# First batch's inverse transform: channel pairs (c, c+128) and whole 128-column weights in its last stage

## The chip, the cores and the metric

The kernel runs on one core of one Trainium2 chip. Inside a core, TensorE (PE) multiplies matrices and writes its results to PSUM; VectorE (DVE) and ScalarE (ACT) work element by element and carry PSUM results to SBUF; GpSimd (POOL) does side work; SyncE (SP) and POOL issue most of the DMAs. The metric is device microseconds of one execution. Before the change three executions took 790.2, 790.48 and 791.0 us, median 790.48 us.

A PE weight load (LDWEIGHTS, shown as its own engine PEld) puts the *stationary* operand into the array; the matmul that follows streams the *moving* operand through it. Both are read from SBUF, each partition along its own row, with a stride that the program chooses.

## The reference, cut to what matters

```
X = np.fft.rfft(x, axis=1)                 # x: 8 batches x 3008 positions x 256 channels
Y = X * (filt_r + 1j * filt_i)
y = np.fft.irfft(Y, n=3008, axis=1)        # per channel: a filter along the positions
h = y.reshape(24064, 256) @ w_in           # 256 -> 2048
s = np.sin(alpha * h)
out = (h + s * s / alpha) @ w_out          # 2048 -> 256
```

## The kernel before, in words

Positions are split as 3008 = 94 x 32, 94 rows (two interleaved sets of 47) by 32 columns that the code calls `n`. The forward transform of a batch is two matrix stages with a turn between them, then comes the product with the filter, then two inverse stages with a turn back between them. The result `y` is held in fp16 as two blocks of 128 channels (`cb` = 0, 1) by positions, and the second half of the kernel consumes it in chunks of 512 positions: `hidden(k, jb)` (L500) does two matmuls (one for each `cb`) with `w1`, ACT takes a sine (L510), DVE makes the snake activation (L511); `project(k, u)` (L515) multiplies by `w2` and stores. 48 such chunks, 12 for every two batches, carry most of the time.

Batches 1 to 7 are spread in small pieces between those matmuls by a list of due times (`put`, L557, and `slot`, L597); their turns go through DRAM by DMA. Batch 0 has to be there before the first chunk, so it is done on the chip by itself, in a written order (L361 to L492). This is the part that the change touches:

- First stage (L368 to L378): 16 matmuls; DVE and ACT in turn copy each result from PSUM into `t1_0`. The copy regroups the 256 channels as 128 pairs, because the turn moves 32-bit words, two fp16 channels at a time. Before the change a pair is (2c, 2c+1).
- Turn (`turn`, L383): four DVE transposes of 32x32 blocks of 32-bit words, into two halves `t2_0[0]` and `t2_0[1]` (`hc` = 0, 1), each with 64 pairs. `t2_0[0]` is the memory `t4_h[0]`. The memory `t4_h[1]` meanwhile holds `e1_0`, the second table of the inverse. In a turned tile the two members of a pair are neighbours, and the next pair of the same `n` or frequency lies 64 elements (128 bytes) further on.
- Second stage (`forward_0`, L399), 12 calls of four matmuls, K=128, 128x128 weights `d_t`, moving operand 128 columns read straight from the turned tile: 64 pairs of neighbours, 128 bytes apart. ACT copies the result to `xf0`.
- Product (`product_0`, L409), one DVE instruction per call on 128 neighbouring channels of the filter, for both filter parts.
- Third stage (`inverse_0`, L416), eight matmuls per call, contiguous moving operands, PSUM pool `fps` with two buffers; ACT copies the result into `g_0` with `(k c) -> c k`, so that here columns c and c+64 of the half become a pair.
- Turn back (`turn_back`, L388), two DVE transposes, of half 0 and then of half 1, into `t4_0[0]` and `t4_0[1]`. As pairs are (c, c+64) inside one half of 128 channels, `t4_0[cb]` has exactly the 128 channels of the block `cb`.
- Last stage (`last(u)`, L246): 16 calls `u`, each for four values of `n` and one `cb`. For batch 0 each `n` takes two matmuls, k = 0 and 1, with 64 weight columns each (stride 128 bytes in SBUF), whose outputs go to PSUM partitions 0 to 63 and 64 to 127. PSUM comes from `fps` again, so two calls can be open. ACT or DVE copies the result (128x376) into `y`.

The order around it, L474 to L492: `reciprocal(rec)` is issued on DVE right behind the two transposes; PE does the two last alpha broadcasts (`spread_alpha`, L295), `warm_pe(2)` (matmuls on zeros that keep the array busy), `last(0)` and `last(2)` (both of `cb` = 0, which need only the first transpose), `warm_pe(3)`, then `last(1)` and `last(3)` (`cb` = 1, which need the second transpose). Then `hidden(0,0)`, `hidden(0,1)` and the transpose of `rec` on PE (L611), whose copy `rec_t` (L612) scales `w2`. Calls 4 to 15 of `last` come in pairs (`last_two`, L262) at the due times 1, 3, 4.5, 6, 14 and 16, between the hidden matmuls of the first three chunks (L571). No DMA is touched by the change.

Of the kernel before, what the change touches and what calls it, by code (L numbers as in the profile page):

```python
# [9 lines left out]
FP16 = mybir.dt.float16  # L10
# [4 lines left out]
ALU = mybir.AluOpType  # L15
# [3 lines left out]
B, S, C = 8, 3008, 256  # L19
# [43 lines left out]
def kernel(  # L63
# [10 lines left out]
    nc = tc.nc  # L74
# [21 lines left out]
    cpool = pool("consts", 1)  # L96
# [12 lines left out]

    wf_t = cpool.tile([NR, NK], FP16)  # L110
    t1_h = [cpool.tile([128, 16, C], FP16, name=f"t1_h{i}") for i in range(2)]
    t4_h = [cpool.tile([128, 16, C], FP16, name=f"t4_h{i}") for i in range(2)]

    def by_half(t):

# [8 lines left out]
    for h in range(2):  # L124
        nc.sync.dma_start(out=x32[:, 4 * C * h:4 * C * h + 4 * C],
                          in_=bass.AP(tensor=x.tensor, offset=x.offset + 4 * h * C, ap=[[32 * C, 96], [1, 4 * C]]))
# [4 lines left out]
    wi0_t = cpool.tile([128, NR], FP16)  # L131
    filt_t = cpool.tile([128, 2, NS, C], FP16)
# [23 lines left out]
    def evac(dst, src, on_act=None):  # L156
        flip[0] = (flip[0] + 1) % 3
        if flip[0] if on_act is None else on_act:
            marks["act"] = nc.scalar.copy(out=dst, in_=src)  # L159
        else:  # L160
            marks["dve"] = nc.vector.tensor_copy(out=dst, in_=src)  # L161

    class Spectral:
# [82 lines left out]
        def last(self, u, on_act=None):  # L246
            ch, rest = divmod(u, 4)
            half, cb = divmod(rest, 2)
            n0 = 8 * ch + 4 * half
            ps = fps.tile([128, 4, 128], FP32, name=f"pd_{self.b}_{u}", tag="f")  # L250
            psv = ps.rearrange("p a b -> p (a b)")[:, 0:4 * NR].rearrange("p (a r) -> p a r", r=NR)
            for i in range(4):
                if self.b == 0:
                    for k in range(2):
                        nc.tensor.matmul(out=psv[64 * k:64 * k + 64, i, :], lhsT=t4_0[cb][:, n0 + i, :, k],  # L255
                                         rhs=wi0_t, start=True, stop=True)
                else:
                    nc.tensor.matmul(out=psv[:, i, :], rhs=wi_t, start=True, stop=True,  # L258
                                     lhsT=t4_h[ch // 2][0:NK, n0 % 16 + i, cb * 128:cb * 128 + 128])
            evac(y[:, cb, self.b % 2, n0:n0 + 4, :], psv, on_act)  # L260
# [9 lines left out]
    al = cpool.tile([16, 128], FP32)  # L270
# [33 lines left out]
    for g in range(2):  # L304
        gs = slice(12 * g, 12 * g + 12)
        for k, filt in enumerate((filt_r, filt_i)):
            for q in range(2):
                if (g, k, q) == (0, 1, 1):
# [3 lines left out]
                    out=f_t[k][64 * k + 32 * q:64 * k + 32 * q + 32, gs, :],  # L312
# [8 lines left out]
    def pairs(t):  # L321

        return t.rearrange("p a (b s k) -> p s (a b) k", s=32, k=2)

    t1_0 = vpool.tile([128, 32, C], FP16, name="t1_0", tag="v")
    t2_0 = [t4_h[0], vpool.tile([128, 16, C], FP16, name="t2_0", tag="v")]
    for hc in range(2):
        nc.vector.memset(pairs(t1_h[hc])[:, NS:32], 0.0)
    t1_0, t2_0, g_0, t4_0 = pairs(t1_0), [pairs(t) for t in t2_0], [pairs(t) for t in t1_h], [pairs(t) for t in t4_h]
    rec = cpool.tile([16, 128], FP32)  # L330
    rec_t = cpool.tile([128, 16], FP32)
# [17 lines left out]
    def warm_pe(n):  # L349

        warmed.append(n)
        ps = hps.tile([128, 512], FP32, name=f"warm_{len(warmed)}", tag="h")
        for i in range(n):
            nc.tensor.matmul(out=ps, lhsT=idle[:, 0:128], rhs=idle[:, 0:512], start=True, stop=True)
# [13 lines left out]
    for i in range(16):  # L368
        own, tag = (fps, "f") if i % 3 == 2 else (hps, "h")
        ps = own.tile([128, 512], FP32, name=f"pa_0_{i}", tag=tag)  # L370
        nc.tensor.matmul(out=ps, lhsT=wf0_t[0:NR], rhs=x0[i // 4][:, 2 * (i % 4):2 * (i % 4) + 2, :],
                         start=True, stop=True)
        evac(t1_0[:, 2 * i:2 * i + 2], ps.rearrange("p (n c k) -> p n c k", n=2, k=2), i % 2)
        if i == 1:
            warm_pe(3)
            cast_x0(1)
        if i < 15 and i % 4 == 3:
            warm_pe((2, 2, 2, 1)[i // 4])  # L378
# [18 lines left out]
    xf0, p0 = {}, {}  # L397

    def forward_0(i):  # L399
        hc, w = blocks[i]  # L400
        ps = hps.tile([128, 4, 128], FP32, name=f"pb_0_{i}", tag="h")
        for j in range(4):
            nc.tensor.matmul(out=ps[:, j, :], lhsT=d_t[:, 4 * w + j, :],
                             rhs=t2_0[hc][:, 4 * w + j], start=True, stop=True)
        own, tag = (xspool, "xs") if i % 2 else (xfpool, "xf")
        xf0[i] = own.tile([128, 4, 128], FP16, name=f"xf_0_{i}", tag=tag)
        nc.scalar.copy(out=xf0[i], in_=ps)

    def product_0(i):  # L409
        hc, w = blocks[i]  # L410
        p0[i] = xpool.tile([128, 2, 4, 128], FP16, name=f"p_0_{i}", tag="x")
        marks["products"] = nc.vector.tensor_tensor(
            out=p0[i], in0=xf0[i][:, None].to_broadcast([128, 2, 4, 128]),
            in1=filt_t[:, :, 4 * w:4 * w + 4, 128 * hc:128 * hc + 128], op=ALU.mult)

    def inverse_0(i):  # L416
        hc, w = blocks[i]
# [53 lines left out]
        if i == 12:  # L471
            turn_back(0)
    turn_back(1)
    nc.vector.reciprocal(out=rec, in_=al)  # L474
    def weights_out(jb, n=4):

        if n == 1:
# [6 lines left out]
    spread_alpha(3)  # L484
    for step in ([(weights_in, g) for g in range(6)] + [(s1.load_x, 0), (s1.load_x, 1)]):
        step[0](*step[1:])
    warm_pe(2)
    s0.last(0, True)
    s0.last(2, True)
    warm_pe(3)  # L490
    s0.last(1, True)
    s0.last(3, False)  # L492

    chunks = [(pb, c0, 384 if c0 == 2560 else 512) for pb in range(B // 2)
              for c0 in [*range(0, 2561, 512), *range(2944, 2 * S, 512)]]
# [167 lines left out]
```

## Time and profile before

| what | value |
|---|---|
| median of the executions shown | 790.48 us |
| profiled execution: span from first to last instruction | 789.0 us |
| what lies around the span, by the median (790.48 - 789.0) | 1.5 us |
| PE busy | 776.2 us, 98% of the span, 5854 matmuls |
| DVE, ACT busy | 657.4 us (83%), 617.0 us (78%) |
| granted TensorE clock | 1.00 |
| second stage of batch 0 (L403) | 48 matmuls, 15.7 to 26 us |
| third stage (L422) | 96 matmuls, 21.5 to 31 us |
| two transposes back (L385) | 30.38 to 34.88 us |
| last stage of batch 0 (L255) | 128 matmuls of 64 columns, 32.7 to 71.3 us |

The span is the time from the program's first instruction to its last in one profiled execution; the profile's own execution is not among the three timed ones, and the 1.5 us is only the difference of the two numbers. Times in the text are counted from the start of the span. A matmul's row gives its own duration, from issue to the modelled end; matmuls overlap, so what an operation takes of the PE is the distance between two starts, which the timeline shows as (total - one duration) / (count - 1). "Idle before, releaser" names what the engine waited for.

### The profile page before, as it was taken

The numbers are of one execution on the slowest core, as the hardware profiler recorded it, in microseconds if no ns is written. First come the engines' busy times: TensorE is split into PE (matmuls) and PEld (weight loads), VectorE is DVE, ScalarE is ACT, GpSimd is POOL, SyncE is SP. The second block draws the span as 40 slices with busy tenths as digits, with TensorE's granted clock in tenths as the row PEclk, the third lists the DMA queues.
The fourth block names the chain that finished last, engine by engine and source line by source line (L and its number), as shares of the span: only waits on it lengthen the run. The fifth ranks groups of instructions, "written<-read, shape, count | busy, mean of one in ns | idle before, by whom it ended". The sixth has DMA issues, their size and how long they took to land.

```text
span 789.0 us, 16730 instructions
## 1 busy us (share of the span) xinstructions
PE 776.2 (98%) x5854; PEld 536.3 (68%) x5854; DVE 657.4 (83%) x1171; ACT 617.0 (78%) x1209; POOL 79.7 (10%) x125
## 2 busy tenths in 40 slices
PE   8999989999999999999999999999999999999997
PEld 4756757676667766777666766777666776766666
DVE  7887987899878997799978998799987999777773
ACT  6887868888878887888887888788887887777663
POOL 6442000200020000200020000200002000000000
PEclk9999999999999999999999999999999999999999
DMA  9956568755573646554575455845566233421111
GB/s 217 257 105 173 118 144 206 173 104 134 140 198 82 135 98 191 150 121 102 121 210 124 100 106 137 219 94 113 128 165 171 62 97 82 116 62 29 41 41 54
DMA packets 87677, 101.01 MB, mean 128 GB/s; under 512 B 14472, under 2 KB 75928, under 8 KB 87592
## 3 DMA queue, kind: packets, MB, share of 16 engines
q1 hardware_dynamic: 78016, 73.73, 34.5%
q0 software_dynamic: 9360, 26.15, 17.4%
q8 instruction: 46, 0.75, 0.4%
q14 instruction: 39, 0.32, 0.1%
q10 hardware_dynamic: 216, 0.05, 0.0%
HBM read 55.72 MB, written 46.66 MB: 130 GB/s over the span
## 4 chain that ended last, share of the span: by engine, by line
PE 90%; DVE 2%; DMA 2%; ACT 2%; issue 1%; POOL 1%; SPq 1%; ACTq 0%; POOLq 0%; DVEq 0%
PE po L523 40%; PE ph L507 40%; PE pa L180 3%; PE pd L258 2%; PE pb L200 2%; PE pc L231 2%; DMA e_t<-e_tbl 1%; DVE v L511 1%; PE pd L255 1%; DMA xs<-xf 1%; ACT cos_all L510 1%; DVE t_h L385 1%; SPq L549 1%; ACT t_h L159 1%; DVE t_h L161 0%
## 5 line engine op out<-in xcount | busy, mean ns | idle before, releaser
L511 DVE SCALAR_TENSOR_TENSOR v<-cos_all,ph 128x512 f16<-128x512 f32 (+1 forms) x768 | 482.8, 671 | 107.4 <-ACT cos_all L510 103.9
L510 ACT ACTIVATE cos_all<-ph 128x512 f32<-128x512 f32 (+1 forms) x768 | 410.9, 592 | 99.5 <-PE ph L507 98.3
L523 PE MATMUL po<-w,v 128*128 128x256 f16 x3008 | 388.7, 272 | 0.0
L507 PE MATMUL ph<-y,w 128*128 128x512 f16 (+1 forms) x1536 | 386.4, 374 | 0.5 <-DVE y L161 0.3
L523 PEld LDWEIGHTS <-v 128*128 128x128 f16 x3008 | 289.3, 98 | 78.2 <-issue 1.2
L507 PEld LDWEIGHTS <-w 128*128 128x128 f16 x1536 | 147.5, 98 | 104.5 <-issue 2.5
L529 ACT COPY o<-po 128x512 f32<-128x512 f32 (+1 forms) x97 | 55.6, 573 | 19.6 <-PE po L523 12.6
L203 ACT CAST xf<-pb 128x512 f16<-128x512 f32 x84 | 50.0, 595 | 15.2 <-PE pb L200 13.8
L192 POOL DMA_DIRECT2D t<-d x56 | 36.3, 666 | 202.4 <-DMA out_dram<-o 128.6
L159 ACT CAST t_h<-pa 96x512 f16<-96x512 f32 x74 | 43.3, 586 | 8.5 <-PE pa L180 8.3
L140 POOL DMA_DIRECT2D x<-in_x_dram x32 | 17.1, 535 | 302.1 <-PE pc L231 171.4
L159 ACT CAST y<-pd 128x376 f16<-128x376 f32 x83 | 40.0, 482 | 7.6 <-PE pd L258 5.3
L258 PEld LDWEIGHTS <-t_h 96*128 96x128 f16 x448 | 31.4, 97 | 18.4 <-issue 0.4
L180 PE MATMUL pa<-x,wf_t 94*96 94x512 f16 x112 | 42.2, 381 | 1.0 <-DVE t_h L161 0.6
L159 ACT CAST g<-pc 128x512 f16<-128x512 f32 x58 | 34.4, 593 | 9.4 <-PE pc L231 9.0
L221 DVE TENSOR_TENSOR p<-p,xs 128x512 f16<-128x512 f16 x84 | 35.7, 425 | 2.9
L220 DVE TENSOR_TENSOR xs<-xs,filt_t 128x512 f16<-128x512 f16 x84 | 35.0, 416 | 2.8 <-DMA xs<-xf 2.8
L258 PE MATMUL pd<-wi_t,t_h 96*128 96x94 f16 x448 | 37.1, 204 | 0.0
L214 DVE TENSOR_TENSOR p<-xf,filt_t 128x512 f16<-128x512 f16 x84 | 35.0, 416 | 0.0
L231 PE MATMUL pc<-p,e_t 128*128 128x256 f16 x168 | 32.1, 273 | 1.7 <-DVE p L221 1.7
L200 PE MATMUL pb<-t,d_t 128*128 128x256 f16 x168 | 32.1, 272 | 0.5 <-DVE g L161 0.4
L161 DVE CAST t_h<-pa 96x512 f16<-96x512 f32 x38 | 25.9, 681 | 0.7 <-PE pa L180 0.5
(66 smaller groups left out, 257.5 us busy)
## 6 DMA issues: line engine op xcount, KB each, us to landing
x<-in_x_dram POOLq DMA_DIRECT2D x30, 376.0 KB, 5.0
d<-t_h SPq DMA_DIRECT2D x28, 384.0 KB
t<-d POOLq DMA_DIRECT2D x56, 192.0 KB, 4.6
xs<-xf SPq DMA_DIRECT2D x168, 64.0 KB
d<-g SPq DMA_DIRECT2D x56, 192.0 KB
t_h<-d SPq DMA_DIRECT2D x28, 384.0 KB
out_dram<-o SPq DMA_DIRECT2D x104, 80.0 KB
w_out<-in_moe_w_out_dram SPq DMA_DIRECT2D x1, 2048.0 KB
```

Source lines behind the costliest of these rows:

```text
L159: marks["act"] = nc.scalar.copy(out=dst, in_=src)
L180: marks["pe"] = nc.tensor.matmul(out=ps[0:NK, :], lhsT=wf_t, rhs=self.x[ch][:, 2 * j:2 * j + 2, :], start=True, stop=True)
L192: nc.gpsimd.dma_start(out=self.t2[g][64 * p:64 * p + 64, :, :], in_=self.d1[a0:a0 + 6, :, :].rearrange("s n c -> n s c"))
L200: nc.tensor.matmul(out=ps[:, i, :], lhsT=d_t[:, s, :], rhs=self.t2[s // 6][:, s % 6, :], start=True, stop=True)
L203: nc.scalar.copy(out=self.xf[u], in_=ps)
L231: nc.tensor.matmul(out=ps[:, i, :], lhsT=e_t[:, 2 * w + i, :], rhs=pt[:, i, :], start=(k == 0), stop=(k == len(pr) - 1))
L258: nc.tensor.matmul(out=psv[:, i, :], rhs=wi_t, start=True, stop=True, lhsT=t4_h[ch // 2][0:NK, n0 % 16 + i, cb * 128:cb * 128 + 128])
L507: nc.tensor.matmul(out=ps[:, 0:n], lhsT=w1[:, cb, jb * 128:jb * 128 + 128], rhs=y_cols[:, cb, c0:c0 + n], start=(cb == 0), stop=(cb == 1))
L510: nc.scalar.activation(out=cs[:, 0:n], in_=ps[:, 0:n], func=AFT.Sin, bias=float(np.pi / 2))
L511: marks["snake"] = nc.vector.scalar_tensor_tensor(out=v[k][:, jb, 0:n], in0=cs[:, 0:n], scalar=-1.0, in1=ps[:, 0:n], op0=ALU.add, op1=ALU. ...
L523: nc.tensor.matmul(out=pso[k][:, t % 2, :], lhsT=v[k][:, jb, 128 * t:128 * t + 128], rhs=w2[:, jb, :], start=(jb == 0), stop=(jb == 15))
L529: nc.scalar.copy(out=o[:, i0:t % 2 + 1, :], in_=pso[k][:, i0:t % 2 + 1, :])
```

## The change

Pairs become (c, c+128) from the first copy on: `t1_0` is filled with `(n k c) -> n c k`. Each half `hc` then has channels 64·hc to 64·hc+63 and the same plus 128, in both `t2_0` and `g_0`. To keep the two members apart as two runs of 64 channels, the second stage reads its moving operand as `(k c)`: first all 64 first members, then all 64 second members, each 128 bytes from the next. The product takes two runs of 64 filter channels in place of one of 128. The third stage and its copy are as before. After the turns back, the member k of all 128 pairs of both halves is the block `cb` = k; the two `t4_h` become halves of one tile `t4_a`, so that 128 columns with a constant stride of 128 bytes can be addressed, and the last stage does one matmul of 128 weight columns per `n` where it did two of 64. Every call of `last` now reads both halves, hence both transposes. The opening order becomes `warm_pe(8)`, `last(0)`, `last(1)`, `last(2)`, `last(3)` with copies by ACT, DVE, ACT, DVE, and the reciprocal moves behind them on DVE.

```
-    t4_h = [cpool.tile([128, 16, C], FP16, name=f"t4_h{i}") for i in range(2)]
+    t4_a = cpool.tile([128, 2, 16, C], FP16)
+    t4_h = [t4_a[:, i] for i in range(2)]
...
                 if self.b == 0:
-                    for k in range(2):
-                        nc.tensor.matmul(out=psv[64 * k:64 * k + 64, i, :], lhsT=t4_0[cb][:, n0 + i, :, k],
-                                         rhs=wi0_t, start=True, stop=True)
+                    nc.tensor.matmul(out=psv[:, i, :], lhsT=t4_cols[:, n0 + i, :, cb], rhs=wi0_t,
+                                     start=True, stop=True)
...
+    t4_cols = t4_a.rearrange("p h a (b s k) -> p s (h a b) k", s=32, k=2)
...
-        evac(t1_0[:, 2 * i:2 * i + 2], ps.rearrange("p (n c k) -> p n c k", n=2, k=2), i % 2)
+        evac(t1_0[:, 2 * i:2 * i + 2], ps.rearrange("p (n k c) -> p n c k", n=2, k=2), i % 2)
...
             nc.tensor.matmul(out=ps[:, j, :], lhsT=d_t[:, 4 * w + j, :],
-                             rhs=t2_0[hc][:, 4 * w + j], start=True, stop=True)
+                             rhs=t2_0[hc][:, 4 * w + j].rearrange("p c k -> p k c"), start=True, stop=True)
...
-            out=p0[i], in0=xf0[i][:, None].to_broadcast([128, 2, 4, 128]),
-            in1=filt_t[:, :, 4 * w:4 * w + 4, 128 * hc:128 * hc + 128], op=ALU.mult)
+            out=p0[i].rearrange("p f s (k c) -> p f s k c", k=2),
+            in0=xf0[i].rearrange("p s (k c) -> p s k c", k=2)[:, None].to_broadcast([128, 2, 4, 2, 64]),
+            in1=filt_t[:, :, 4 * w:4 * w + 4].rearrange("p f s (k c) -> p f s k c", k=2)[..., 64 * hc:64 * hc + 64],
+            op=ALU.mult)
...
     turn_back(1)
-    nc.vector.reciprocal(out=rec, in_=al)
...
-    warm_pe(2)
-    s0.last(0, True)
-    s0.last(2, True)
-    warm_pe(3)
-    s0.last(1, True)
-    s0.last(3, False)
+    warm_pe(8)
+    for u in range(4):
+        s0.last(u, u % 2 == 0)
+    nc.vector.reciprocal(out=rec, in_=al)
```

## The prediction

> **What bounds the kernel now.** I read the page's busy times and its chain first, then the chain of waits from 20 to 38 us, the timelines of PE and DVE around the places that the diff names, and last the rows of single lines. Busy times, and the chain by engine:
>
> ```profile
> PE 776.2 (98%) x5854; PEld 536.3 (68%) x5854; DVE 657.4 (83%) x1171; ACT 617.0 (78%) x1209; POOL 79.7 (10%) x125
> PE 90%; DVE 2%; DMA 2%; ACT 2%; issue 1%; POOL 1%; SPq 1%; ACTq 0%; POOLq 0%; DVEq 0%
> ```
>
> PE sets the end almost everywhere, so what is won or lost before batch 0 is ready, or in the first chunks, moves everything behind it. The chain around batch 0 (start, length, what):
>
> ```profile
> 11.77 9.71 DMA e_t<-e_tbl
> 21.48 0.05 issue
> 21.53 0.64 PE pc L422 x8
> ...
> 26.06 0.69 ACT t_h L159
> 26.75 0.48 ACT xf L407
> 27.23 0.53 ACT t_h L159
> ...
> 30.38 4.51 DVE t_h L385 x2
> 34.89 0.04 issue
> 34.94 1.23 PE pd L255 x16
> 36.16 0.02 issue
> 36.19 0.56 DVE y L161
> ```
>
> To see here: until 21.5 us a transfer decides, then ACT's copies with PE close behind, then the two transposes back, then the last stage. PE in that stretch (start, length from first start to last end):
>
> ```profile
> 15.70 1.49 PE L403 MATMUL pb<-t_h,d_t 128*128 128x128 f16 x12
> 17.69 1.04 PE L354 MATMUL warm<-idle 128*128 128x512 f16 x4
> 19.05 1.50 PE L403 MATMUL pb<-t,d_t 128*128 128x128 f16 x12 [0.32 <-DVE t L385]
> 20.37 0.62 PE L403 MATMUL pb<-t_h,d_t 128*128 128x128 f16 x4
> 21.53 0.23 PE L422 MATMUL pc<-p,e_t 128*128 128x128 f16 x1 [0.54 <-DMA e_t<-e_tbl]
> 21.60 0.22 PE L422 MATMUL pc<-p,t_h 128*128 128x128 f16 x1
> ```
>
> L403 has 128 moving columns like L422, but its starts are (1.49 - 0.29)/11 = 110 ns apart against 55 for L422 (21.60, 21.65, 21.71): the moving operand in 64 separate pairs costs twice the contiguous one. That is 1.72 ns for each separate place. The rows of the weight loads and of the last stages (min/median/max):
>
> ```profile
> L343 PEld LDWEIGHTS <-d_t x48: 106/110/110, 14.4 to 17.5; 128*64 128x64 f16 x48
> L255 PEld LDWEIGHTS <-t_h x128: 187/221/235, 32.7 to 71.2; 128*64 128x64 f16 x128
> L258 PEld LDWEIGHTS <-t_h x448: 95/97/100, 129.4 to 731.5; 96*128 96x128 f16 x150
> ```
>
> ```profile
> 41.67 1.18 PE L255 MATMUL pd<-wi_t,t_h 128*64 128x94 f16 x16
> 42.78 1.04 PE L507 MATMUL ph<-y,w 128*128 128x512 f16 x4
> 43.75 0.69 PE L255 MATMUL pd<-wi_t,t_h 128*64 128x94 f16 x8
> 45.01 0.68 PE L255 MATMUL pd<-wi_t,t_h 128*64 128x94 f16 x8 [0.56 <-ACT y L159]
> 129.50 0.33 PE L258 MATMUL pd<-wi_t,t_h 96*128 96x94 f16 x4
> ```
>
> The same 64 columns load in 110 ns contiguous and in 221 strided. The 64-column matmuls go two by two, a pair about every 125 ns ((1.18 - 0.3)/7); the contiguous 128-column last stage of other batches needs (0.33 - 0.20)/3, about 41.
>
> **The change part by part.**
>
> *Second stage, moving operand in 128 single places (L403).* No row shows a moving operand of single elements. Below it lies today's 110 ns (twice as many separate places cannot cost less), above it 128 places x 1.72 = 220. I take 220, because the row that is nearest, single columns of the weight load L255, pays about 125/64 = 1.95 ns per single element, no less than a pair does here. That is +0.44 us per call of four. Step by step: calls 0 to 2 end 1.3 us later, at 18.3; the 16 table transposes (0.5) and four warm matmuls (0.86) behind them now end at 19.7, so call 3 starts 0.65 later than 19.05. Calls 3 to 6 add 1.76: the first inverse starts at 23.2, not 21.53 (the 0.7 us that PE idles from 20.8 for the table's DMA are used up). Calls 7 to 11 stand between inverses 0 to 5 and add 2.2: inverse 5 is 3.9 late. ACT copied it 0.43 after PE had it, behind its own queue, and that slack goes: 3.4 late. From there the two `fps` buffers pace inverses 6 to 11 as before, so both transposes are 3.4 late: **+3.4**, or 0 at 110 ns. DVE's products (685 ns) stay hidden: the last operand arrives near 30.2, its inverse is due near 33.8.
>
> [...]
>
> *Copy of the first stage, product, one tile.* The strided PSUM read of the copy is already in ACT's L159 of the third stage, 636 ns mean against 655 for today's copy: nothing. DVE's copy has no such row; as the loads of x pace the copies, only the last before the transposes would count, 0 to 0.2, taken as 0. DVE's product keeps its 1024 elements, in runs of 64 in place of 128: nothing; even 0.1 more each would stay behind PE, as above. I see no way to a gain in either. If the two halves in one tile were ordered as one, the transpose of half 0 would wait for the last read of `e1_0` at 30.8: +0.5, unlikely, since other tiles are used by halves now.
>
> *Weights of 128 strided columns.* No row has them. From below 41 ns per matmul (L258, contiguous). From above 128 x 1.95 = 250, every column behind the other. Between them 125, what the two halves side by side take now. I take 62, a quarter of 250: in the trace's operands all 128-column fp16 loads are four groups of 32 columns, and they take 97 ns where 64 contiguous ones take 110, so the groups go side by side, as the two halves do.
>
> [...]
>
> *Opening order.* Now: second transpose ends at 34.88, the second-block hidden matmul starts at 36.79, 1.9 later; `last(0)` and `last(2)` were done beside the transpose. Then, with 0.5 us from a call's first matmul to its last result, 0.045 per semaphore step, ACT 0.47 and DVE 0.55 a copy: `last(0)` done 0.54, copied 1.06; `last(1)` done 0.82, copied 1.42; `last(2)` waits for the first buffer, 1.11 to 1.60; `last(3)` for the second, 1.46 to 1.96, copied by DVE at 2.55; hidden at 2.60. **+0.7**. The reciprocal (0.90) now stands on DVE behind that copy and ends at 3.4; PE's transpose of it (L611), which came 2.67 behind, waits for it, and `hidden(0,2)` behind that: +0.2 on PE; DVE's first snake is later anyway. `rec_t` then comes near 43.3 and POOL's first `w2` piece (43.08) slips 0.3, used only by the first projections (now 51.2). Eight warm matmuls (1.7) end 1.0 before the second transpose: hidden. PE then waits for it with all hidden matmuls queued behind, as it does now. No DMA moves and SP's queue is untouched. Together **+0.8**.
>
> *Twelve calls in the loop.* Six places, from the hidden matmul before to the next instruction after: 1.25, 1.21, 1.96, 1.27, 1.21, 1.19, sum 8.1 us. A place of eight matmuls at 62 ns and 0.15 for entry and exit is 0.65. The two at 65.6 and 70.3 lie on a gapless PE: 2 x 0.55 = 1.1. Of the four in the first chunk DVE and ACT take part back:
>
> ```profile
> 41.11 2.48 DVE L511 SCALAR_TENSOR_TENSOR v<-cos_all,ph 128x512 f16<-128x512 f32 x4 [0.24 <-ACT cos_all L510]
> 43.51 0.54 DVE L161 CAST y<-pd 128x376 f16<-128x376 f32 x1
> 44.05 1.28 DVE L511 SCALAR_TENSOR_TENSOR v<-cos_all,ph 128x512 f16<-128x512 f32 x2
> ```
>
> DVE works without a gap from 41.1 to 45.3. Followed engine by engine, the next hidden matmuls come 0.53, 1.03 and 1.3 earlier behind the first three places; the fourth gives nothing, since ACT runs without a gap from 46.3 to 50.6 (sines and four `w2` pieces). So 1.3 of 4 x 0.55: **-2.4** in all; -2.7 at 41 ns, -0.2 at 125, +5.1 at 250.
>
> **Sum**: 3.4 + 0.8 - 2.4 = +1.8 us, on a span of 789.0 with 1.5 around it to the median 790.48: 792.3.
>
> **The rivals.**
> - *Single elements cost no more than pairs* (110 ns). For it: both are separate reads, and two weight loads at once might be slowing each other in L255. Against: L255's 1.95 ns per element. Then +0.8 - 2.4 = -1.6: 788.9, faster. It decides below about 180 ns per matmul, where the loss falls under 1.6 us.
> - *The strided 128-column load gains nothing over two halves* (125 ns): the two halves may already share one path. The loop gives 0.2, the opening costs 1.4 and the wait for the reciprocal 0.2: 3.4 + 1.6 - 0.2 = +4.8: 795.3.
> - *It goes column by column* (250 ns): 3.4 + 3.3 + 5.1 = +11.8: 802.3. Against it is the 97 ns of the contiguous load.
> - *The second stage is hidden anyway* under the table's DMA: it hides only the 0.7 counted above.
>
> **How the numbers follow.** Forecast (220 and near 62) 0.42, its own range, for loads from 41 to 90 ns, 791.4 to 793.7. 125 ns: 0.17. 250 ns, with either price of the second stage: 0.14. Pairs' price with fast weights: 0.12. A price near 165 for the second stage (nine calls x 0.22 less the slacks 0.7 and 0.43, so +0.9 - 1.6, 789.8) or pairs' price with 125 ns (0 + 1.6 - 0.2, 791.9): 0.15. The range 788.8 to 797 leaves out the 250 case and the edge of the fast one, under 2 in 10. 0.2%, 1.6 us, is about what a measurement of this kernel can tell. Faster than that: about half of the fast case and what I may have missed, 0.12. Within it: the other half, two fifths of the forecast, part of the last group, 0.30. Slower: the rest, 0.58.
>
> **What would show it.** Starts of L403 about 220 ns apart and the first L422 near 23.2; transposes from 33.8 to 38.3; weight loads of the new last stage near 140 ns and matmuls 62 apart; L611 waiting for the reciprocal; pairs in the loop 0.65 long. I am wrong if L403 stays near 110, if the new weight loads exceed 200 ns, or if DVE and ACT give back less than I follow.

## The result and the profile after

The changed kernel takes 798.17 us (median; 795.52 to 802.89) where the kernel before takes 790.82 in the same comparison: ratio 1.0090, 95% interval 1.0065 to 1.0114. A second comparison, `after_again` below, gives 1.0071 (1.0049 to 1.0094). So it is slower by 5.6 to 7.1 us by the ratios; 1.8 was forecast. The range's upper end, 797.0, lies between the two medians, 798.17 here and 795.75 there. The profiled execution is the slowest of the first comparison: 802.89 us, span 801.1.

The page's busy times, and its chain by engine:

```profile
PE 782.6 (98%) x5793; PEld 537.0 (67%) x5793; DVE 658.8 (82%) x1172; ACT 617.9 (77%) x1208; POOL 79.8 (10%) x125
...
PE 87%; DMA 4%; DVE 3%; ACT 2%; issue 1%; SPq 0%; POOL 0%; ACTq 0%; POOLq 0%; DVEq 0%
```

There are 61 fewer matmuls (64 saved, three warm ones added), yet PE is busy 6.4 us longer, and DMA's share of the chain has doubled. The chain of waits shows where (start, length, what):

```profile
20.98 3.48 PE pb L404 x16
24.47 0.45 PE pc L425 x8
24.92 0.86 PE pb L404 x4
25.78 0.85 PE pc L425 x8
26.63 0.85 PE pb L404 x4
27.48 0.86 PE pc L425 x8
28.34 0.85 PE pb L404 x4
...
35.58 4.52 DVE t_a L386 x2
...
42.31 1.94 PE ph L507 x4
```

The second stage is on the chain without a break from 20.98 us, where before a transfer decided until 21.5. Four of its matmuls take 0.86 us. The inverses behind them should all take 0.45; two take 0.85. PE's timeline around the same places (start, length, and in brackets the idle time before):

```profile
20.82 2.77 PE L404 MATMUL pb<-t,d_t 128*128 128x128 f16 x12
...
25.79 0.31 PE L425 MATMUL pc<-p,e_t 128*128 128x128 f16 x1
25.89 0.31 PE L425 MATMUL pc<-p,t_a 128*128 128x128 f16 x1
...
29.14 0.22 PE L425 MATMUL pc<-p,e_t 128*128 128x128 f16 x1
29.20 0.22 PE L425 MATMUL pc<-p,t_a 128*128 128x128 f16 x1
...
40.14 0.92 PE L255 MATMUL pd<-wi_t,t_a 128*128 128x94 f16 x8 [0.87 <-DVE t_a L386]
```

Single elements: (2.77 - 0.38)/11 = 217 ns from start to start, against 110 for pairs. Contiguous inverses: 55 ns apart at 29.2 us, 105 at 25.8. The windows of busy time explain that (PE and the four other engines with their instruction counts, then granted clock, DMA share, GB/s):

```profile
22.00:26.00 4.00, 4.00 (x28) 2.47 (x27) 2.40 (x5) 2.93 (x6) 0.00 (x0) 0.90 0.61 132
26.00:30.00 4.00, 4.00 (x33) 3.06 (x32) 3.28 (x5) 2.97 (x6) 0.00 (x0) 0.67 0.94 251
```

The granted clock falls to 0.67 while PE shows no gap (4.00 of 4.00). These are means over 4 us; from 26 to 28 us alone it is 0.50. The new last stage, weight loads and matmuls (min/median/max):

```profile
L255 PEld LDWEIGHTS <-t_a x64: 167/217/243, 40.1 to 76.2; 128*128 128x128 f16 x64
L255 PE MATMUL pd<-wi_t,t_a x64: 202/266/287, 40.1 to 76.2; 128*128 128x94 f16 x64
```

128 strided columns load in about the 221 ns that 64 took, and eight matmuls in 0.92 us start some 92 ns apart ((0.92 - 0.28)/7), where a pair of halves took 125. In the loop they start 82 to 86 ns apart. Last, PE's waits from 60 to 160 us (total, times, longest):

```profile
PE pb L201 <- DMA t<-d: 3.1, 1, 3.1
PE pd L258 <- DMA t_a<-d: 2.5, 1, 2.5
```

Neither wait is in the kernel before. Both are batch 1's: `t` is its `t2`, read back from `d1` in DRAM at 77 us, `t_a` its `t4`, read back from `d2`. The waits also cost more than their length. From the chain, and from the windows of busy time:

```profile
77.01 5.10 DMA t<-d
...
83.59 1.71 PE po L523 x8
...
87.12 0.87 PE po L523 x8
```

```profile
84.00:88.00 4.00, 4.00 (x22) 2.40 (x20) 2.52 (x5) 1.90 (x4) 0.00 (x0) 0.67 0.30 68
```

Eight projection matmuls take 1.71 us behind the wait and 0.87 a little later; the clock is 0.67 from 84 to 88 us, and 0.66 from 140 to 144, behind the wait for `t_a`.

### The profile page after: what moved, and what is told of

It is laid out like the page before. It is cut to its first block, busy times and chain, and to the rows that moved or that the text cites. A ratio compares the mean times of both kernels' runs of the same rounds, so it can differ in the third digit from the quotient of the medians.

```text
span 801.1 us, 16608 instructions
## 1 busy us (share of the span) xinstructions
PE 782.6 (98%) x5793; PEld 537.0 (67%) x5793; DVE 658.8 (82%) x1172; ACT 617.9 (77%) x1208; POOL 79.8 (10%) x125
## 4 chain that ended last, share of the span: by engine, by line
PE 87%; DMA 4%; DVE 3%; ACT 2%; issue 1%; SPq 0%; POOL 0%; ACTq 0%; POOLq 0%; DVEq 0%
PE po L523 38%; PE ph L507 37%; PE pa L181 3%; PE pd L258 2%; PE pb L201 2%; PE pc L232 2%; DVE v L511 2%; DMA id<-id 1%; PE pb L404 1%; ACT cos_all L510 1%; DMA out_dram<-o 1%; DMA t<-d 1%; DMA d<-t_h 1%; DVE t_a L386 1%; PE pc L425 1%
## 5 line engine op out<-in xcount | busy, mean ns | idle before, releaser
L258 PEld LDWEIGHTS <-t_a 96*128 96x128 f16 x448 | 31.3, 97 | 20.9 <-DMA t_a<-d 2.7
L258 PE MATMUL pd<-wi_t,t_a 96*128 96x94 f16 x448 | 37.1, 204 | 2.5 <-DMA t_a<-d 2.5
L162 DVE CAST y<-pd 128x376 f16<-128x376 f32 x46 | 25.0, 543 | 4.5 <-PE pd L258 3.0
```

## Where the time goes, stage by stage

For the experiments I set each profile against the one of before, by the start of six instructions: the first transpose back (30.38 us in before); the fifth hidden matmul, which begins the second block (37.71); the projection's matmuls 64, 80, 264 and 328, counted from 0 and called po64 and so on (71.51, 75.21, 124.92, 141.40); and the end of the span (789.0). Each cell is what a stretch adds or takes, in us:

| stretch | after_again | before_singles | before_opening | pairs_read | pairs_open | pairs_clear | singles_clear |
|---|---|---|---|---|---|---|---|
| to the transposes | +5.73 | +3.79 | +1.79 | -0.26 | -0.05 | -0.02 | +4.56 |
| opening | +0.92 | -0.04 | +1.50 | +1.49 | +0.53 | +0.51 | +0.54 |
| loop, to po64 | -2.56 | -0.05 | -0.05 | -1.93 | -1.35 | -1.34 | -1.33 |
| to po80 (`t2` of batch 1) | +1.56 | 0 | 0 | +2.00 | 0 | 0 | 0 |
| to po264 | -1.89 | -1.83 | -0.52 | -1.07 | -1.66 | -1.95 | -1.31 |
| to po328 (`t4` of batch 1) | +3.54 | 0 | +0.01 | +0.17 | +2.52 | +0.01 | +0.01 |
| to the end | -0.51 | -0.50 | +0.54 | -0.52 | -0.50 | -0.52 | -0.51 |
| sum | +6.78 | +1.37 | +3.26 | -0.12 | -0.52 | -3.30 | +1.96 |

A column is one execution, and executions of one kernel differ by several us; the ratios below come from many. The column of `after_again` is that kernel's slowest (797.6 us against a median of 795.75).

The stretch to po264 falls in every column because a wait of the kernel before is shorter there; what shortens it is open, so a gain in that row can't be put down to a column's edit. In the profile of before DVE's cross product waits for a transfer, and PE for DVE:

```profile
116.09 0.42 DVE L220 TENSOR_TENSOR xs<-xs,filt_t 128x512 f16<-128x512 f16 x1 [2.83 <-DMA xs<-xf]
```

## Experiments: which edit costs what

**after_again**: the changed kernel unchanged, beside the three that follow.

> The changed kernel once more, for a second profile and more executions. If its loss is regular: a median of 797 to 799 us against 790 to 791, the second stage's matmuls 217 ns apart, and the granted clock under 1 in two places, behind the second stage's slow matmuls (21 to 30 us) and around the opening calls of the last stage (38 to 50 us). If much of the profiled 12 us was one bad execution: the first cast of x on DVE at 4.9 us as before, not at 5.7, and a span of 795 to 797 us with fewer waits for DMA after 80 us.

795.75 us, ratio 1.0071 (1.0049 to 1.0094). The loss is real.

**pairs_read**: the changed kernel with the old order of reading in the second stage; ACT's copy then does the reordering.

```diff
-    rhs=t2_0[hc][:, 4 * w + j].rearrange("p c k -> p k c")
+    rhs=t2_0[hc][:, 4 * w + j]
-  nc.scalar.copy(out=xf0[i], in_=ps)
+  nc.scalar.copy(out=xf0[i].rearrange("p s (k c) -> p s k c", k=2),
+                 in_=ps.rearrange("p s (c k) -> p s k c", k=2))
```

> The changed kernel, but the second stage reads its moving operand as pairs of neighbours again, and ACT's copy puts the columns in order. If the single-element reads are the main loss (3.4 us by the forecast, and the clock behind them): 790 to 792.5 us, matmuls 110 ns apart, transposes back from about 30.4 us, clock 1.00 from 21 to 30 us. If the last stage's strided weights and the opening order are the main loss: 795 us or more.

790.38 us, ratio 1.0006 (0.9991 to 1.0021): 0.0065 less than `after_again`, 5.1 us. So the single elements carry nearly all of the loss, about 3 to 7 us with both intervals. The other edits ahead of the transposes (first copy, product, one tile) cost nothing there that shows: the table has -0.26. But the rest isn't the gain of 1.6 that the other terms add up to. Its waits from 50 to 160 us show one reason:

```profile
PE pb L201 <- DMA t<-d: 1.8, 1, 1.8
```

**before_singles**: the kernel before with single elements in the second stage alone; ACT's copy restores the old order.

```diff
-    rhs=t2_0[hc][:, 4 * w + j]
+    rhs=t2_0[hc][:, 4 * w + j].rearrange("p c k -> p k c")
+  # copy: out "p s (c k) -> p s k c", in "p s (k c) -> p s k c"
```

> The kernel before, with only the second stage's moving operand read as single elements (64 first members, then 64 second ones; ACT's copy puts them back). If these reads are the main loss: 794 to 796 us, matmuls 217 ns apart, transposes back 3.4 us late or more, the clock under 1 behind them. If they are hidden or the loss is elsewhere: 790.5 to 791.5 us.

794.64 us, ratio 1.0052 (1.0033 to 1.0071), that is 4.1 us (2.6 to 5.6). Its timeline, and its windows:

```profile
21.79 1.04 PE L403 MATMUL pb<-t,d_t 128*128 128x128 f16 x4
22.66 1.05 PE L403 MATMUL pb<-t_h,d_t 128*128 128x128 f16 x4
23.53 0.24 PE L423 MATMUL pc<-p,e_t 128*128 128x128 f16 x1
23.60 0.22 PE L423 MATMUL pc<-p,t_h 128*128 128x128 f16 x1
```

```profile
22.00:26.00 4.00, 4.00 (x32) 2.56 (x31) 2.34 (x5) 3.63 (x6) 0.00 (x0) 1.00 0.44 106
```

0.87 us a call of four at full clock; the transposes are 3.79 late, with nothing else changed but the order in ACT's copy (744 ns each in place of 620). The profiled execution is the fastest of the eight (792.16, against a median of 794.64), so it shows the edit without a drop of the clock: five of the eight have a mean clock of 0.998 or less, four of the 25 of the kernel before beside them. (In the changed kernel's profile the 0.90 and 0.67 of the windows from 22 to 30 us come to 3.4 us at 0.50, which takes 0.002 off the mean.)

**before_opening**: the kernel before with the changed kernel's opening (eight warm matmuls, then the four calls, the reciprocal behind them); the calls keep 64-column halves.

```diff
-    warm_pe(2)
-    s0.last(0, True)
-    s0.last(2, True)
-    warm_pe(3)
-    s0.last(1, True)
-    s0.last(3, False)
+    warm_pe(8)
+    for u in (1, 0, 3, 2):
+        s0.last(u, u % 2 == 1)
+    nc.vector.reciprocal(out=rec, in_=al)
```

> The kernel before with only the opening order changed as in the change: eight warm matmuls, four calls that all stand behind the second transpose (in the order 1, 0, 3, 2, as call 1 needs it), the reciprocal behind their copies; weights stay in halves of 64 columns. By the forecast 1.4 for the calls and 0.2 for the reciprocal: 792 to 792.8 us. If the opening is hidden: 790.8 us. If a clock drop in the wait adds to it, the clock is under 1 between 36 and 50 us and the time 793 to 795 us.

793.14 us, ratio 1.0038 (1.0023 to 1.0052), 3.0 us. The opening takes 1.50 longer in the table, where the prediction's rival of 125 ns said 1.4 and 0.2. In this execution the first inverse was also 1.23 later than in before, behind a wait of 1.57 us for the table's transfer, and the clock was 0.76 and 0.81 in the two windows from 22 to 30 us. Ten of its twelve executions have a mean clock of 0.998 or less, against 4 of 25 of the kernel before beside them, so a drop is a likely part of the other 1.5 us of the ratio; that is not tested.

## Experiments: batch 1's round trip

First theory: in the kernel before, the calls 12 to 15 fill PE's time while batch 1 goes through DRAM; shorter calls leave PE waiting for `t2`.

**pairs_fill**, **before_fill**, **after_fill**: `pairs_read`, before and after with two more calls moved into that time.

```diff
-  put((1,3,4.5,6,14,16)[u // 2 - 2], s0.last_two, u, pe=True)
+  put((1,3,4.5,13.5,14.5,16)[u // 2 - 2], s0.last_two, u, pe=True)
```

> The changed kernel with pairs read back in the second stage (as in pairs_read), and the calls 10 and 11 of batch 0's last stage moved from step 6 to step 13.5, behind batch 1's loads of t2. Theory (the shorter calls no longer fill PE's time in batch 1's round trip through DRAM, so PE waits for t there): PE's wait for the t2 load falls from 1.8 us by about one place, 0.65, to about 1.1; the projection po80 comes about 0.6 earlier than in pairs_read, and if nothing later swallows it the time is 789.8, against 790.4 of pairs_read. Rival (the gain is swallowed by the later waits of batch 2, near 110 us, whatever stands in the round trip): po80 earlier, but po264 and the end unchanged, 790.4.

789.91 us, ratio 0.9998 (0.9981 to 1.0015). The wait for `t` is gone altogether, which is more than the theory asked for: the transfer itself was quicker in this execution (3.6 us from the last store to `d1` to the first load of `t2`, 5.05 in `pairs_read`), for a reason that the section on the instruction fetch finds. The time differs from that of `pairs_read` by less than the intervals.

> The kernel before with the same move of calls 10 and 11 to step 13.5. Theory: the kernel before shows no wait for t there, so there is nothing to fill; PE's work is only moved, 790.5, ratio 1.000 within 0.15%. Rival (the new place is worth something by itself, for instance because the first chunk's stage gets shorter): 0.5 to 1 us faster.

791.89 us, ratio 1.0032 (1.0017 to 1.0046): slower, which neither expectation had. PE waits 1.7 us for `t_h` at 130 us, the wait of the changed kernel.

> The changed kernel with nothing but the move of calls 10 and 11 to step 13.5. Theory: as in pairs_fill, the wait for t falls by about 0.65 and the time from 795.75 to about 795.1; the second stage's single elements keep their 3.7 and more, so it stays slower than before by 0.5% or more. Rival (the round trip holds most of the loss, as the waits for t, 1.4 to 3.1, and for t_a, 1.9 to 2.5, come to 3 to 5 us): 792 or less.

794.97 us, ratio 1.0060 (1.0039 to 1.0081). Near the theory's 795.1; the rival's 792 is out.

**pairs_open**: `pairs_fill` with an opening without buffer waits and without gaps on PE.

```diff
-    warm_pe(8)
+    warm_pe(12)
     for u in range(4):
-        s0.last(u, u % 2 == 0)
+        s0.last(u, u % 2 == 0, *((hps, "h") if u > 1 else ()))   # pool of the result buffer
+    warm_pe(3)
```

> pairs_fill with the opening mended: calls 2 and 3 take their result buffers from the hidden stage's pool, so that they don't wait for the copies of calls 0 and 1, and 12 warm matmuls ahead of the four calls and 3 behind them in place of 8 ahead, so that PE has no gap. Theory (the opening's loss of 1.5 is the buffer wait, and the half clock behind it comes from PE's gaps): the first hidden matmul comes 0.3 to 0.5 earlier than in pairs_fill, the first eight hidden matmuls go at full clock and end 1 us earlier, some of which ACT and DVE give back; the time 0.5 to 1 below pairs_fill, near 789.0, ratio 0.998. Rival (the copies of ACT and DVE set the opening, and they or batch 1's transfers take up what PE wins): as pairs_fill within 0.3.

789.49 us, ratio 0.9989 (0.9976 to 1.0002). PE's timeline of the opening, first of `pairs_read`, then of `pairs_open`:

```profile
34.68 0.92 PE L255 MATMUL pd<-wi_t,t_a 128*128 128x94 f16 x8 [0.87 <-DVE t_a L386]
35.80 0.92 PE L255 MATMUL pd<-wi_t,t_a 128*128 128x94 f16 x8 [0.20 <-ACT y L160]
36.83 1.97 PE L508 MATMUL ph<-y,w 128*128 128x512 f16 x4
38.73 0.28 PE L612 MATMUL ps_rec<-id,rec 16*128 16x16 f32 x1
```

```profile
34.89 1.65 PE L255 MATMUL pd<-wi_t,t_a 128*128 128x94 f16 x16
36.36 0.82 PE L355 MATMUL warm<-idle 128*128 128x512 f16 x3
37.02 1.03 PE L509 MATMUL ph<-y,w 128*128 128x512 f16 x4
38.02 0.23 PE L613 MATMUL ps_rec<-id,rec 16*128 16x16 f32 x1
```

The same four hidden matmuls take 1.97 us behind an opening with gaps (granted clock 0.79 from 36 to 44 us) and 1.03 behind one without (1.00). The opening's stretch falls from 1.49 to 0.53, and the lead grows to 2.5 us at po264. Then it is lost again, on the wait for `t4`:

```profile
PE pd L258 <- DMA t_a<-d: 2.3, 1, 2.3
```

SP's queue shows why. First `pairs_open`, then the kernel before; `d<-g` are the last stores to `d2`, the loads to `t_a` or `t_h` the first of `t4`:

```profile
117.26 1.25 SPq L239 DMA_DIRECT2D d<-g  x2
119.29 0.32 SPq L186 DMA_DIRECT2D d<-t_h  x1
125.61 1.68 SPq L244 DMA_DIRECT2D t_a<-d  x3
```

```profile
118.07 1.25 SPq L238 DMA_DIRECT2D d<-g  x2
121.82 0.32 SPq L185 DMA_DIRECT2D d<-t_h  x1
122.32 2.81 SPq L243 DMA_DIRECT2D t_h<-d  x3
```

In `pairs_open` the stores are issued earlier and the load, which waits for them to land (5.9 us for `d<-g`, by SP's waits), comes later. POOL issues the fourth load of batch 2's x (376 KB) at 117.95 there, 0.07 us behind the last store, and at 120.49, 1.8 behind it, in the kernel before. In all 20 profiles of this study it is the same: with that load within 0.1 us of the store, `t4` is issued 6.8 to 7.7 us behind the store (after, `after_again`, `pairs_open`, `before_fill`); with it 0.6 us behind or later, 3.0 to 3.6 (the other 16).

**after_load**, **before_load**, **pairs_load**: after, before and `pairs_open` with that load three steps later. **after_all**: `pairs_load` with single elements.

```diff
-  put((22,27,32,37)[ch] if b == 2 else z - 92 + 7 * ch, s.load_x, ch)
+  put((22,27,32,40)[ch] if b == 2 else z - 92 + 7 * ch, s.load_x, ch)
```

> The changed kernel with one transfer moved: the fourth load of batch 2's x, 376 KB, from step 37 to step 40. In ten profiles the first load of batch 1's t4 is issued 6.8 to 7.7 us behind the last store of d2 where that load of x is issued within 0.1 us of the store (changed kernel twice, pairs_open, before_fill), and 3.0 to 3.6 where it comes 0.9 to 1.8 later. Theory (the load of x takes the transfer engines from the store, and the last stage of batch 1 waits for it): t4 about 3 to 3.6 behind the store, PE's wait for t_a of 1.9 to 2.5 gone, and of the 3.5 to 4 us that the changed kernel loses between the projections po264 and po328 at least 3 come back: 792 to 793, ratio 1.003. Rival (the store is late for another reason, its own queue or its small pieces, and the load of x only goes with it): 6.8 to 7.7 stay, 795.5.

796.33 us, ratio 1.0083 (1.0070 to 1.0096). The first part of the theory holds: 3.0 us from store to load, where the four profiles named above have 6.8 to 7.7, and no wait for `t_a`. The gain doesn't come: x is too late at its new place (PE waits 1.2 us for it), and the wait for `t` is 2.8 in this profile.

> The kernel before with the same load moved from step 37 to step 40. Theory: its load comes 1.8 us behind the store already, so nothing changes: 790, ratio 1.000 within 0.15%. Rival (the later place is worth something by itself, or some executions of the kernel before meet the same collision): 1 us or more faster.

791.06 us, ratio 1.0021 (1.0009 to 1.0032): slower, with a wait of 1.4 us for x. Step 40 was a poor choice.

> pairs_open with the same load moved to step 40. Theory (the 2.5 us that pairs_open is ahead at the projection po264 were lost to the same collision, a wait of 2.3 for t_a): the lead stays to the end, 787.0 to 787.8, ratio 0.997, faster than the kernel before. Rival (another transfer of batch 1 is late next, as its whole chain of transfers moves with its own stages): 789, ratio 0.999.

791.51 us, ratio 1.0016 (1.0002 to 1.0031). 3.05 us from store to load, but a wait of 1.6 for x, and 1.7 for `t`, which `pairs_open`, the same program up to there, didn't have.

> pairs_load with nothing but the second stage's moving operand as in the changed kernel, single elements at 217 ns a matmul. Theory (what the prediction summed for this edit holds by itself when no transfer is met on the way): 3.4 to 4.6 us slower than pairs_load, 3.4 of the sum plus up to 0.9 where two inverses run at half clock; near 791.3. Rival (most of the loss of the changed kernel lies in the collisions that the later start runs into, and batch 1's waits take the rest up): less than 2 us slower than pairs_load.

794.49 us, ratio 1.0062 (1.0049 to 1.0074); 0.0046 above `pairs_load`, 3.6 us. That is inside what the theory asked for.

## Experiments: the instruction fetch

What makes `t` late in one execution and not in another? The trace's DMA packets of the kind "instruction" fall into two queues; q8 has blocks of 16 KB, one for about every 250 matmuls and weight loads of PE (46 blocks for 5854 matmuls and as many weight loads in the kernel before). In the kernel before one starts at 58.9 us and the next at 77.0. With 122 PE instructions fewer (61 matmuls and their weight loads; the expectation below says 128), in `after_again` one starts at 71.4, in the middle of the last store to `d1` (issued at 70.42). Over the 20 profiles:

| fetch behind the issue of d1's last store | profiles | from that store to the first load of t2 |
|---|---|---|
| 0.98 to 1.74 us | after, after_again, after_load, after_all, pairs_read, pairs_load, before_fetch2 | 4.3 to 5.5 us |
| none near, or 2.3 us and more | the other 13 | 3.5 to 3.9 us |

**before_fetch**: the kernel before with warm matmuls cut into narrower ones, which adds instructions and hardly any PE time (24 of 256 columns take 2.78 us in `pairs_clear`, 12 of 512 took 2.75 in `pairs_open`), so as to pull the fetch of 77.0 to the store. **after_fetch**: the changed kernel with 64 more matmuls made the same way. **after_clear**: `after_fetch` with the load of x at step 38. **pairs_clear**: `pairs_open` with both.

```diff
-        for i in range(n):
-            nc.tensor.matmul(out=ps, lhsT=idle[:, 0:128], rhs=idle[:, 0:512], start=True, stop=True)
+        for i in range(n):
+            for k in range(parts):   # 3 in after_fetch, 4 in before_fetch
+                cs = slice(512 * k // parts, 512 * (k + 1) // parts)
+                nc.tensor.matmul(out=ps[:, cs], lhsT=idle[:, 0:128], rhs=idle[:, cs], start=True, stop=True)
```

> The kernel before with its warm matmuls cut into smaller ones of the same total width (four of 128 columns for one of 512; 75 more matmuls, 150 more PE instructions, no more PE time). Theory (PE's instructions are fetched by the DMA engines in blocks of 16 KB; a fetch that falls 1 to 1.7 us behind the last store of d1 delays its landing; the changed kernel has 128 PE instructions fewer, so its fetch moved there from 58.9): the extra instructions pull the fetch of 77.0 forward to near 66.5, 1 to 1.7 us behind the store of d1 at 65.3; the first load of t2 comes 4.3 to 5.5 us behind the store in place of 3.5 to 3.9, PE waits 0.5 to 2 us for t, and the time grows by 0.5 to 2 us. Rival (the fetch only goes with something else in the changed kernel, for instance the 128-column places that end sooner): 3.5 to 3.9 stay, no wait for t, 790 within 0.5.

789.88 us, ratio 0.9990 (0.9975 to 1.0005). The fetch came 2.6 us behind the store, past the place aimed at; 3.9 to `t2`. It decides nothing.

> The changed kernel with its warm matmuls cut in three (64 more matmuls, as many PE instructions as in the kernel before, no more PE time). Theory: the fetch goes back from 71.4 to near 62, clear of d1's store; t2 3.5 to 3.9 behind the store, the wait for t of 1.4 to 3.1 gone, and the projection po80 is as late as po64, about 4.1, in place of 5.6 to 8; the collision at d2's store may stay, so the end gains 1 us or nothing. Rival: the wait for t stays, as the shorter places leave it open.

794.72 us, ratio 1.0054 (1.0030 to 1.0077). The fetch is away from the store, `t2` 3.9 behind it, and PE waits 0.7 for `t` in place of 1.4. What is left may be the filler that the shorter calls no longer give; this run doesn't separate it.

> after_fetch with the fourth load of batch 2's x at step 38 in place of 37 (40 came too late: PE waited 1.2 for it). Theory (the two collisions are what the prediction's sum lacked): no wait for t and none for t_a; late by about 4.1 at po64 and po80, by about 2.2 at po264 and at the end: 792 to 793, which is the forecast. Rival (the loss is in the terms of the sum): 794.5 or more.

795.08 us, ratio 1.0055 (1.0038 to 1.0071). Neither collision occurs (3.9 and 3.6 us), and still it isn't the forecast: the rival's number holds. The transposes are 4.69 late, the opening costs 1.49, PE waits 1.0 for `t`, and the kernel before's wait near 110 is back with 1.3. So the collisions are not all that the sum lacked: this ratio lies 0.0016 (1.3 us) under that of `after_again`, 3.5 us at most with the two intervals, and 3.8 are to be explained.

> pairs_open with the warm matmuls cut (60 more) and the fourth load of batch 2's x at step 38. Theory: neither wait, t2 3.5 to 3.9 and t4 about 3 us behind their stores; the 2.5 us ahead of the kernel before at po264 stay to the end: 787.5, ratio 0.997. Rival (a third transfer is late next): 789 or more.

788.8 us, ratio 0.9971 (0.9957 to 0.9985): faster than both kernels. The lead at po264 stays to the end, as the theory said. But 1.95 of the table's 3.3 us lie in the stretch to po264, and no run gave the kernel before the same opening, places, narrow warm matmuls and load of x together: how much of the lead is the new last stage's is not shown. Its busy times:

```profile
PE 773.9 (99%) x5860; PEld 540.6 (69%) x5860; DVE 658.5 (84%) x1173; ACT 615.5 (78%) x1207; POOL 80.0 (10%) x125
```

**before_fetch2**: `before_fetch` with ten more narrow matmuls in the opening. **singles_clear**: `pairs_clear` with single elements, the diff of `pairs_read` backwards.

```diff
-    warm_pe(2, 1)
+    warm_pe(2, 3)
...
-    warm_pe(3, 2)
+    warm_pe(3, 4)
```

> before_fetch with ten more of the small warm matmuls (the last two calls cut in three and four), so that the fetch comes about 1.6 us earlier: in before_fetch it came 2.6 us behind the last store of d1, where it delayed nothing (3.9 to t2). Theory: the fetch about 1.0 behind the store, t2 4.3 to 5.5 behind it, PE waits for t 0.5 to 1.5 us. Rival (the fetch delays nothing by itself): 3.5 to 3.9, no wait.

The fetch starts 1.05 us behind the store, which is issued at 65.57; 4.51 us to `t2`, and PE waits for it. From the DMA view between the store's issue and that load, from POOL's queue, and from the waits:

```profile
q8 instruction: 1, 0.02, 1.4%
```

```profile
70.08 5.22 POOL L192 DMA_DIRECT2D t<-d  x8 [20.90 <-DMA d<-t_h]
```

```profile
PE pb L200 <- DMA t<-d: 1.0, 1, 1.0
```

Against `before_fetch` (2.6 us behind, 3.9) nothing is new in this kernel but ten more narrow warm matmuls, and so the instruction count. So the place of the fetch brings the delay, as far as one profile of each can show it. It is worth nothing in the end, though: 789.2 us, ratio 0.9998 (0.9986 to 1.0009). Where the 1.1 us lost at po80 go is not settled; the stretch to po264 gains 2.05, which is hardly more than in columns that lost nothing.

> pairs_clear with nothing but the second stage's moving operand as in the changed kernel, single elements. Theory (the price of this edit is its own 3.4 to 3.8 us and up to 0.9 for a half clock, the rest of the changed kernel's loss lies elsewhere): 3.4 to 4.7 slower than pairs_clear's 788.8 at the same distance to the kernel before, ratio to before 1.0015 to 1.0030. Rival (a later batch 0 costs more than its own time, as batch 1's transfers then meet others): ratio 1.005 or more.

793.36 us, ratio 1.0054 (1.0037 to 1.0071), 0.0083 above `pairs_clear`: 6.6 us, and 4.8 at the least with the two half-widths, 0.0017 and 0.0014, taken together. The rival's ratio is nearer. In the two profiles the distance is 5.3 us: 4.6 at the transposes, where the clock is 0.64 from 22 to 26 us, and 0.6 near 110 us, none of it a wait for a transfer of batch 1; what more there is in the 6.6 is not located, and the two kernels come from different comparisons. All six executions have a mean clock of 0.998 or less, none of the twelve of `pairs_clear`. Four pairs of kernels now price the single elements: 4.1, 5.1, 3.6 and 6.6 us, each within 1.5 to 2.1 either way, and all above the 3.4 of the sum.

## Why the prediction was wrong, point by point

- *Second stage in 128 single places: 220 ns.* Right: 217 measured, and 110 for pairs, 55 for contiguous operands in these traces: pairs pay, and singles pay twice as much again.
- *+3.4 at the transposes.* The first of two steps that failed: 3.79 alone, 4.10 to 5.73 in the changed kernel and its kin (`after_fill` 4.10, `after_load` 4.45, `after_again` 5.73). A part of these numbers is only when the second stage starts in that execution (15.45 to 16.68 us). From its first matmul to the first transpose back it is 14.68 us in before; with single elements it is 18.20 and 18.25 at full clock (`after_fetch`, `before_singles`), 18.9 in six profiles with a drop of the clock, and 20.15 in `after_again`. So at full clock the edit costs 3.5 to 3.6, and the working was right to 0.2. What it put at nothing is the granted clock, which it didn't consider because it is 1.00 in the trace of before. A drop adds 0.7: two inverses take 0.85 in place of 0.45. In `after_again` the low clock lasts longer and adds 1.9. Its rows, and one of its windows:

```profile
18.65 1.07 PE L344 MATMUL pse<-id,d_t 128*64 128x128 f16 x16
19.65 1.89 PE L355 MATMUL warm<-idle 128*128 128x512 f16 x4
21.33 2.80 PE L404 MATMUL pb<-t,d_t 128*128 128x128 f16 x12
```

```profile
22.00:26.00 4.00, 4.00 (x24) 2.70 (x23) 0.75 (x2) 2.46 (x5) 0.00 (x0) 0.50 0.38 93
```

- *The clock, further.* At 0.50 the contiguous matmuls take nearly twice as long (four warm ones 1.89 us in place of 1.04), but the single elements stay 218 ns apart, as at full clock. The clock is below 1 between 22 and 30 us in seven of nine profiles with single elements; in all seven PE is busy for 4.00 of 4.00 us in each of the three windows from 18 to 30 us. With pairs it is two of eleven (`before_opening`, `before_fetch`), both behind a gap of over 1 us (1.57, 1.08). What makes the clock fall behind a PE without gaps was not tested.
- *The 0.7 us that PE idled for the table.* The working spent them as slack, and they belonged to some executions only. In six profiles with pairs the first inverse starts between 20.49 (`before_load`) and 20.95 us (`pairs_open`), not at 21.53; there the way to the transposes is 14.24 to 14.48 us, and the price of single elements 3.7 to 4.0. So the slack hid 0.2 to 0.4 of the price, not 0.7.
- *Weights of 128 strided columns: 62 ns, loads near 140.* Too fast: about 92 ns in the opening, 82 to 86 in the loop, and loads of 217, over the 200 that the prediction named as a sign of being wrong; in the trace these loads, too, are four groups of 32 columns. It is between the bounds, and better than the 125 of the halves.
- *Opening: +0.8.* 0.92 at full clock; 1.49 where the clock was low behind the gaps. The wait of the reciprocal's transpose for the reciprocal didn't show: it starts straight behind the hidden matmuls.
- *Twelve calls in the loop: -2.4.* Right as far as it went: -2.56, -1.86 (first comparison) and -1.93 up to po64. That it holds with slower matmuls is in part luck: five of the six places take 0.66 to 0.69 us where 0.65 was forecast, because the 0.15 for entry and exit hardly shows. The second step that failed is "PE sets the end almost everywhere, so what is won or lost before batch 0 is ready, or in the first chunks, moves everything behind it". Between 71 and 141 us batch 1's transfers decide as well, and PE's gain turns into waits for them: 1.4 and 3.1 for `t`, 1.9 and 2.5 for `t_a` in the two profiles of the changed kernel, with a low clock behind three of them. In `pairs_read` that leaves +0.0006 where the terms without the second stage say -1.6 us. Where the waits are taken away and the opening is mended (`pairs_clear`), the whole comes out 0.29% ahead of the kernel before; what part of that is the last stage's own is not shown.
- *No DMA moves.* None does in the program. But with 122 PE instructions fewer the fetches start elsewhere (58.9 and 77.0 us in before, 71.4 in `after_again`), and a PE that is earlier or later moves each transfer against its neighbours (batch 2's load of x is 1.8 us behind `d2`'s store in before, 0.07 in `pairs_open`).
- *The rivals.* 795.3, for loads that gain nothing, lies on the measured 795.75, but not for its reasons: the matmuls are 92 ns apart, not 125, and the loop gave 2 us up to po64, not 0.2. Column by column (250 ns) is out as well.

As a whole: from `pairs_read` to `after_again` 5.1 us come with the single elements, of which 3.4 were forecast; opening and loop together, forecast as -1.6, came to about +0.5 (-0.7 to +1.7). What stays open: why the second comparison's 5.6 us were 7.1 in the first (there the profiled execution's first loads landed 1 us late, the wait for `t` was 3.1, and the clock was low behind both waits); what makes the wait near 110 us longer or shorter; and the last 1 to 2 us between the stage table and the ratio in `before_opening` and `singles_clear`.

## What to carry to other kernels

Price a TensorE moving operand by the separate places that it is read from (here 1.7 ns each: 110 ns for 64, 217 for 128), and when a stage becomes slow to feed, price the contiguous matmuls behind it at a lower granted clock too (here 0.50, where eight take 0.85 us in place of 0.45; the clock fell in seven profiles of nine). Before a gain on the busiest engine is carried to the end, follow the transfers that leave and come back through DRAM: what fills the engine meanwhile, and which other transfer starts close behind the store that a load waits for (here a load of 376 KB within 0.10 us, a fetch of 16 KB 0.98 to 1.74 us behind). A slack read from one execution, such as a transfer that lands last, is not a slack that can be spent in full (here 0.2 to 0.4 us of 0.7).

## What the runs showed that I had not expected

- Where a 16 KB instruction fetch started 0.98 to 1.74 us behind a 384 KB store, the load that waits for the store was issued 4.3 to 5.5 us behind it, and 3.5 to 3.9 in the other profiles (4.51 in `before_fetch2`, 3.9 in `before_fetch`). PE's list of waits names no wait for a fetch; what is late is a neighbouring transfer.
- Where a 376 KB load was issued 0.01 to 0.10 us behind a store, the load that waits for the store was issued 6.8 to 7.7 us behind it; at 0.6 us and more, 3.0 to 3.6.
- Strided weights of 128 columns load in 217 ns and go 82 to 92 ns apart, where contiguous ones took 97 ns and 41.
- Single-element matmuls keep their 217 to 218 ns at half clock (0.50 from 22 to 26 us in `after_again`); only the contiguous ones around them slow down.
- The same four 512-column matmuls took 1.97 us behind a PE with gaps of 0.2 to 0.9 us, and 1.03 behind one kept busy.
